# Three-stage kernel (attention, ELU block, gated block): order of products in the ELU block's Strassen pairs, weight-stream steps, token sums and gate differences

## The chip, the cores and the metric

One Trainium2 chip, one core of it. The metric is device time in microseconds (us), the median of several executions. The time of the kernel before is 675.72 us (median of 3 runs, 674.67 to 677.73).

## The reference

Three stages, all in float32:

- Attention with pooled queries: q, k, v are (2, 8, 1152, 64). Pairs of query rows are averaged, scores are scaled by 1/8, softmax, times v. The result, reshaped, is x with 1152 tokens of 512 features.
- First block ("MoE 1" in the kernel's names): h = x @ w_in (512 to 2048), g = h where h > 0, else exp(h) - 1, x2 = g @ w_out (2048 to 512).
- Second block ("MoE 2"): xn = x2 / rms(x2) * rms_g, out = (silu(xn @ w_gate) * (xn @ w_val)) @ w_out, with 1536 inner features.

## The kernel before, in words

**Split numbers.** TensorE multiplies numbers of reduced precision, so each operand is kept as a high part and a lower part (the number minus its high part), and each product is three matmuls: high by high, low by high, high by low (`product`, lines 216 to 218, and `Branch.group`, line 746). A high part is made by a cast, mostly on ACT; a lower part by a subtraction, on POOL (`lo_pool`, line 64) or DVE (`lo_dve`, line 70).

**Chunks and Strassen pairs.** Tokens are taken in three chunks of 384 columns (c = 0, 1, 2). For a pair of 128-wide weight blocks, chunks 0 and 1 together are one 2 by 2 block product done with seven half-depth products (numbers 1 to 7 in `Branch.m`, six matmuls each, line 746), and chunk 2 is done plainly (numbers 8 and 9, one for each weight block, twelve matmuls each). Several products add up in one PSUM bank: 2 goes on top of 1 (bank `a`), 7 and 4 on top of 6 (bank `b`), 3 on top of 5 (bank `e`). Between them a reader must have taken the intermediate value: after 1, ACT copies `a` to m1 (line 758) before 2 may write; after 6, DVE makes u2 = b + m1 (line 781); after 7, DVE makes u3 = b + m1 (line 787) before 4 may write. Products 5, 6, 7, 3 use sums of the weight blocks (s(1) to s(4), from `get_sums`), products 5, 6, 7, 4 use sums of the token blocks (`ts[0]` to `ts[3]`, made from t1, t2, t3, t4).

**Banks.** `bank()` hands out seven PSUM banks in turn, so an allocation waits for the readers of the one seven before it.

**First block.** 16 blocks of w_in and 16 of w_out, in four quarters q. Quarter 0 makes its four w_in blocks with plain products; quarters 1 to 3 are two Strassen pairs each, `Elu(2q)` and `Elu(2q + 1)`, run in an order written out by hand (`run`). Each output goes through `elu`: on ACT a relu (line 246) and an exp (line 247), on DVE a combination (line 248), on ACT a cast (line 249), on POOL the lower part. The last ones are put off by two and three calls of `flush`. After each quarter come rows m = 0 to 3 of w_out (`out1`), each for three chunks, whose results DVE adds into x2 (lines 855, 859).

**Weight stream.** `Stream.work` is a generator, and every `ws.step(i, k)` issues its next k steps between other work, so its place in the engines' queues is set by these counts. For each weight block of 512 KB: ACT takes its two words (line 120, which needs the load; line 122), ACT casts the block before (line 183), POOL makes that one's lower part, DVE puts the words together (lines 131, 133, 136). Line 136 frees a load buffer, of which there are two; SP starts the next load there. After the second block of a pair, POOL makes four sums (lines 156 to 162), ACT casts them (line 170) and POOL makes their lower part. A block has nine steps, a pair of blocks some six more.

**Token sums.** During quarter 0 `sums_from_x` makes the four differences on DVE (line 661), the casts on ACT (line 664), and the lower parts: of t1 and t4 on DVE, of t3 and t2 on POOL.

**Second block.** `Norm.sums`, `spread` and `scale` normalise a chunk (line 717 is a square root on ACT, 718 a reciprocal on DVE, 724 a transpose on TensorE, 730 to 732 scale, cast and split). The first pair of gate and value blocks is done plainly, as `unit(i, c)`: TensorE runs unit(0, 0), unit(1, 0) with the sums of chunk 2, unit(0, 1), the spread of chunk 2, unit(1, 1), unit(0, 2), unit(1, 2). `swiglu` follows a unit with Silu on ACT (line 930) and a product on DVE (line 932). Before the first Silu, ACT loads the table (line 948). The four gate differences t1, t3, t2, t4 are all made on DVE at line 939, right after unit(0, 0) is issued, and three casts (line 941) right after them. Ten Strassen pairs `Gate(2)` to `Gate(11)` follow, then w_out.

The order around the changed place in the second block, before:

```python
    for o, a, b in ((t1, b12, b11), (t3, b22, b12), (t2, b22, t1), (t4, b21, t2)):
        V.tensor_tensor(out=o, in0=a, in1=b, op=ALU.subtract)
    for n, t in ((2, t3), (1, t2), (3, t4)):
        T.copy(ts[n][0], t)
    lo_pool(ts[2][1], t3, ts[2][0])
    ws.step(wi, 4)
    first.append(unit(1, 0, norms[2].sums))
```

Of the kernel before, what the change touches and what calls it, by code (L numbers as in the profile page):

```python
# [12 lines left out]
ALU = mybir.AluOpType  # L13
# [26 lines left out]
def tile_kernel(ctx: ExitStack, tc: tile.TileContext, qd, kd, vd, w1d, w2d, wgd, wvd, wod, rgd, outd):  # L40
    nc = tc.nc
    V, G, T, PE, SP = nc.vector, nc.gpsimd, nc.scalar, nc.tensor, nc.sync
# [20 lines left out]
    def lo_pool(o, i, h):  # L63
        G.tensor_tensor(out=o, in0=i, in1=f(h), op=ALU.subtract)  # L64
# [4 lines left out]
    def lo_dve(o, i, h):  # L69
        V.tensor_tensor(out=o, in0=i, in1=f(h), op=ALU.subtract)  # L70
# [372 lines left out]
    def emit_x(p, xs, a=0, b=QS):  # L443
# [7 lines left out]
        else:  # L451
# [5 lines left out]
    wi = 0  # L457
    ge = tuple(gep.tile([128, NE, CH], F32R, name=f"ge{n}", tag=f"ge{n}") for n in "hl")
    ws = Stream([w for q in range(4) for w in w_in[4 * q:4 * q + 4] + w_out[4 * q:4 * q + 4]]
                + [w[2 * i + n] for i in range(6) for w in (wgd, wvd) for n in range(2)] + [wod[i] for i in range(12)])  # L460
# [31 lines left out]
    for n in range(ns):  # L492
        p, k = n // NPT, n % NPT
# [8 lines left out]
    t = ap.tile([128, 3, 384], F32, tag="p", name="rawq0", bufs=3).rearrange("p a b -> p (a b)")  # L502
    t = t.rearrange("p (u c) -> p u c", u=2)
# [75 lines left out]
    for step in range(ns):  # L579
# [25 lines left out]
        for u in jobs.get(step, []):  # L605
# [4 lines left out]
            n = order.index(u)  # L610
# [40 lines left out]
    def sums_from_x():  # L651

        r = x2.rearrange("p m c -> p (m c)")[:, NT:NT + 3072].rearrange("p (n k c) -> p n k c", n=4, k=2)
        b11, b12, b21, b22 = (r[:, n] for n in (0, 1, 3, 2))
        for b, j, l in ((b11, 0, 0), (b21, 1, 0), (b12, 0, 1), (b22, 1, 1)):
            h, x = (f(t[:, 2 * j:2 * j + 2, cs(l)]) for t in (xh, xl))
            V.tensor_tensor(out=b, in0=h, in1=x, op=ALU.add)
            yield
        t1, t2, t3, t4 = b11, b22, b12, b21
        for n, o, a, b in ((0, t1, b12, b11), (2, t3, b22, b12), (1, t2, b22, t1), (3, t4, b21, t2)):  # L660
            V.tensor_tensor(out=o, in0=a, in1=b, op=ALU.subtract)
            yield
        for n, t in ((0, t1), (2, t3), (1, t2), (3, t4)):
            T.copy(ts[n][0], t)
            yield
            (lo_dve if n in (0, 3) else lo_pool)(ts[n][1], t, ts[n][0])
            yield

    sums_of_x = sums_from_x()
# [143 lines left out]
    def run(order, limit, k=1):  # L813
        ws.limit = limit
        for br, m in order:
            br.m(m)
            ws.step(wi, 3 * k if m > 7 else k)
# [3 lines left out]
    wi = 0  # L821
    for i in range(4):
# [9 lines left out]
                next(sums_of_x)  # L832
        wi += 1

    for q in range(4):
        if q:
            old, b = None, Elu(2 * q)
            run([(b, k) for k in ((1, 8, 2, 9, 6, 5, 7) if q == 1 else (1, 6, 5, 8, 7, 2, 9))], 2 * q + 2)
            old, b = b, Elu(2 * q + 1)
            run([(b, 1), (old, 4), (b, 8), (old, 3)], 2 * q + 2)  # L840
            wi += 2
            run([(b, k) for k in ((9, 6, 5, 7, 2, 4, 3) if q == 1 else (6, 5, 2, 7, 9, 4, 3))], 2 * q + 3)
            ws.limit = 2 * q + 4
            wi += 2

        def out1(c, m, b, then=None, ks=range(4)):
            product(b, ws.get(8 * q + 4 + m), lambda k: g_block(c, k), True, True, ks)
            flush()
            if then:
                then()  # L850
            if ks[-1] < 3:
                return
            x = x2[:, m, cs(c)]
            if q:
                V.tensor_tensor(out=x, in0=b, in1=x, op=ALU.add)
                if q == 3:
                    norms[c].square(m)
            else:
                V.tensor_copy(x, b)

        if q < 3:
            banks = {}
            for m, ks in ((0, (0, 1)), (1, (0, 1)), (0, (2, 3)), (1, (2, 3)), (2, range(4)), (3, range(4))):
                for c in (2, 0, 1):
                    if (m, c) not in banks:
                        banks[m, c] = bank()
                    out1(c, m, banks[m, c], None, ks)
                    if q == 0 and (m, ks[0]) != (1, 2):
                        next(sums_of_x, None)
                        if (m, ks[0]) != (0, 0):  # L870
                            next(sums_of_x, None)
                    ws.step(wi, 6 if len(ks) > 2 else 4 if ks[0] else 3 * m)
                if ks[-1] == 3:
                    wi += 1
        else:
            banks = {}
            for n, (c, m) in enumerate([(0, 0), (0, 1), (0, 2), (0, 3), (1, 0), (1, 1)]):
                b = banks[c, m] = bank()
                out1(c, m, b, None, (0, 1))
                if n == 3:  # L880
                    T.activation(out=dummy, in_=eps, func=AF.Sqrt)
                ws.step(wi, 0 if n < 3 else 2)
            for c in range(3):
                for n in range(4):
                    b, ks = (banks[c, n], (2, 3)) if (c, n) in banks else (bank(), range(4))
                    out1(c, n, b, norms[c - 1].sums if c and n == 3 - c else None, ks)
                    if (c, n) in ((2, 0), (2, 3)):
                        norms[n > 0].spread()
                        norms[n > 0].scale()
                    ws.step(wi, ((2, 2, 2, 0), (1, 1, 3, 3), (3, 3, 3, 3))[c][n])  # L890
            wi += 4
# [28 lines left out]
    def unit(i, c, between=None):  # L920
        b = bank(), bank()
        for n in range(2):
            product(b[n], ws.get(2 * n + i + wi), xchunk(c), True, True)
            if between and n == 0:
                between()
        return i, c, *b

    def swiglu(i, c, pg, pv, k=4):
        s = u[c][:, i]
        T.activation(out=s, in_=pg, func=AF.Silu)  # L930
        ws.step(wi, k)
        V.tensor_tensor(out=s, in0=pv, in1=s, op=ALU.mult)
# [2 lines left out]
    first = [unit(0, 0)]  # L935
    b11, b12, b21, b22 = (x2[:, 2 * j:2 * j + 2, cs(l)] for j in range(2) for l in range(2))
    t1, t2, t3, t4 = b11, b22, b12, b21
    for o, a, b in ((t1, b12, b11), (t3, b22, b12), (t2, b22, t1), (t4, b21, t2)):
        V.tensor_tensor(out=o, in0=a, in1=b, op=ALU.subtract)  # L939
    for n, t in ((2, t3), (1, t2), (3, t4)):  # L940
        T.copy(ts[n][0], t)
    lo_pool(ts[2][1], t3, ts[2][0])
    ws.step(wi, 4)
    first.append(unit(1, 0, norms[2].sums))
# [2 lines left out]
    u = [up.tile([128, 12, CH], F32, name=f"u{c}", tag=f"u{c}") for c in range(2)]  # L947
    T.activation(out=dummy, in_=eps, func=AF.Silu)  # L948
    swiglu(*first[0], 2)
    lo_pool(ts[1][1], t2, ts[1][0])  # L950
    swiglu(*first[1], 3)
    units = [unit(0, 1)]
    norms[2].spread()
    norms[2].scale()
# [38 lines left out]
    b = Gate(2)  # L993
    run([(b, 1), (b, 8), (b, 9), (b, 2)], 2, 4, 2)
    run([(b, 6), (b, 5)], 2, 4)
    old, b = b, Gate(3)
    run([(b, 1), (old, 7)], 2, 4)
    for n in range(3, 11):
        if n > 3:
            old, b = b, Gate(n)  # L1000
            run([(b, 1), (old, 4), (b, 6), (old, 3)], n - 1, n + 2)
        else:
            run([(b, 6), (old, 4), (old, 3)], n - 1, n + 1)
        if n == 10:
            split_u(0, 0, 3)
        run([(b, k) for k in (5, 8, 7, 2, 9)], n, n + 3)
    old = b
    b = Gate(11)
    run([(b, 1), (old, 4), (b, 6), (old, 3)], 10, 12, 1)
# [86 lines left out]
```

## Time and profile before

| what | value |
|---|---|
| median of 3 runs | 675.72 us |
| the profiled execution, its time | 675.94 us |
| its span, first to last instruction | 674.2 us |
| TensorE (PE) busy | 661.6 us, 98% |
| VectorE (DVE) busy | 512.0 us, 76% |
| ScalarE (ACT) busy | 464.7 us, 69% |
| GpSimd (POOL) busy | 448.2 us, 66% |
| mean granted TensorE clock | 0.997 |

Times in the trace count from the span's start. Each line of a timeline has the start, the duration, the engine, the line of the kernel, the operation, output and inputs by the program's names, how many were merged, and in brackets how long the engine sat idle before it and what ended that. Matmul durations overlap, since matmuls are pipelined: the distance of two starts is what one costs. SP is the engine that starts the loads.

### The profile page before, as it was taken

Reading aid. Unit: us, or ns where it says so; the run is one execution under the profiler, and the core shown is the slowest. Engines: PE = TensorE matmul, PEld = TensorE weight load, DVE = VectorE, ACT = ScalarE, POOL = GpSimd, SP = SyncE. Lnnn points to the kernel's source line nnn. Section 1 sums busy time; section 2 is a strip of 40 time slices with the busy share of each in tenths; the row PEclk is TensorE's granted clock in tenths of the full one; section 3 lists DMA queues with packets and bytes.
Section 4 is the critical chain, followed back from the end, with each engine's and each line's share of the span. In section 5 each row is a group of like instructions: output and inputs, shape, how many; then the busy total and the mean of one; then the engine's idle time right before and its main releaser. Section 6 shows DMA issues by size and latency. Waiting matters only on the chain.

```text
span 674.2 us, 11387 instructions
## 1 busy us (share of the span) xinstructions
PE 661.6 (98%) x4149; PEld 652.9 (97%) x4149; DVE 512.0 (76%) x882; ACT 464.7 (69%) x910; POOL 448.2 (66%) x408
## 2 busy tenths in 40 slices
PE   8999999999999999989999999998999999999997
PEld 7999999999999999989999999998999999999997
DVE  7989989998999878886776877678687776776300
ACT  6888889898989868757758658755657654654300
POOL 5998898898988225876685785656979765413200
PEclk9999999999999999998999999999999999999999
DMA  5523333223233002142142241210323322204200
GB/s 175 181 94 96 138 126 112 90 89 120 89 123 103 1 1 95 38 150 90 66 134 87 73 147 62 68 59 32 124 95 126 126 72 84 94 1 142 85 36 35
DMA packets 21624, 61.75 MB, mean 92 GB/s; under 512 B 2752, under 2 KB 5056, under 8 KB 21568
## 3 DMA queue, kind: packets, MB, share of 16 engines
q1 hardware_dynamic: 21568, 61.03, 27.1%
q8 instruction: 32, 0.52, 0.3%
q14 instruction: 24, 0.20, 0.1%
HBM read 58.66 MB, written 2.36 MB: 91 GB/s over the span
## 4 chain that ended last, share of the span: by engine, by line
PE 50%; DVE 3%; ACT 2%; DMA 1%; issue 0%; DVEq 0%; ACTq 0%; SPq 0%
PE b L746 17%; PE b L216 11%; PE b L218 11%; PE b L217 11%; DMA wr<-in_w_dram 1%; DVE x L939 1%; DVE xl L70 1%; ACT xh L731 0%; DVE wt L136 0%; ACT we L120 0%; ACT wm L122 0%; DVE wm L133 0%; DVE wm L131 0%; ACT sqm L707 0%; ACT L948 0%
## 5 line engine op out<-in xcount | busy, mean ns | idle before, releaser
L64 POOL TENSOR_TENSOR wl<-wt,wh 128x512 fp32r<-128x512 f32 x68 | 91.5, 1347 | 75.0 <-ACT wh L183 73.9
L70 DVE TENSOR_TENSOR ptl<-t,pth 128x384 fp32r<-128x384 f32 x216 | 106.7, 548 | 5.0 <-ACT pth L375 4.4
L353 DVE TENSOR_SCALAR_CACHE_REDUCE p<-s 128x1152 f32<-128x1152 f32 x72 | 97.3, 1353 | 14.5 <-PE s L349 13.6
L375 ACT CAST pth<-t 128x384 fp32r<-128x384 f32 x216 | 89.1, 487 | 21.9 <-PE t L367 21.1
L349 PE MATMUL s<-kd,qt 128*128 128x384 f32 x480 | 98.6, 342 | 2.3 <-DVE p L353 1.8
L358 ACT ACTIVATE p<-p,st 128x1152 f32<-128x1152 f32 x72 | 91.4, 1270 | 0.5 <-DVE p L353 0.2
L216 PE MATMUL b<-xh,wh 128*128 128x384 f32 x260 | 88.4, 340 | 1.1 <-ACT u L930 1.1
L218 PE MATMUL b<-xh,wl 128*128 128x384 f32 x260 | 88.1, 339 | 0.0
L217 PE MATMUL b<-xl,wh 128*128 128x384 f32 x260 | 88.0, 339 | 0.0
L349 PEld LDWEIGHTS s<-kd,qt 128*128 128x128 f32 x480 | 81.0, 188 | 5.9 <-DVE p L353 2.5
L393 PE MATMUL o<-pth,vd 128*128 128x256 f32 (+1 forms) x288 | 84.4, 315 | 0.0
L367 PE MATMUL t<-ident,p 128*128 128x128 f32 x648 | 82.5, 273 | 0.0
L393 PE MATMUL o<-ptl,vd 128*128 128x256 f32 (+1 forms) x288 | 78.5, 295 | 0.0
L367 PEld LDWEIGHTS t<-ident,p 128*128 128x128 f32 x648 | 75.0, 141 | 2.0 <-ACT p L358 0.3
L120 ACT ACTIVATE we<-wr 128x512 uint32<-128x512 uint32 x68 | 45.4, 667 | 40.6 <-DMA wr<-in_w_dram 19.8
L131 DVE TENSOR_SCALAR wm<-wm 128x512 f32<-128x512 f32 x63 | 43.7, 694 | 20.3 <-ACT wm L122 20.3
L122 ACT ACTIVATE wm<-wr 128x512 f32<-128x512 f32 x63 | 39.4, 626 | 22.2 <-DVE wt L136 22.2
L393 PEld LDWEIGHTS o<-pth,vd 128*128 128x128 f32 x288 | 54.4, 189 | 0.3
L393 PEld LDWEIGHTS o<-ptl,vd 128*128 128x128 f32 x288 | 54.5, 189 | 0.0
L64 POOL TENSOR_TENSOR gl<-eg,gh 128x384 fp32r<-128x384 f32 x35 | 37.6, 1090 | 21.3 <-ACT gh L249 21.2
L216 PEld LDWEIGHTS b<-xh,wh 128*128 128x128 f32 x260 | 49.4, 190 | 1.4 <-ACT u L930 1.4
L217 PEld LDWEIGHTS b<-xl,wh 128*128 128x128 f32 x260 | 49.4, 190 | 0.0
(194 smaller groups left out, 1765.8 us busy)
## 6 DMA issues: line engine op xcount, KB each, us to landing
wr<-in_w_dram SPq DMA_DIRECT2D x32, 512.0 KB, 3.2
rawq<-in_q_dram SPq DMA_DIRECT2D x15, 576.0 KB, 4.1
rawk<-in_k_dram SPq DMA_DIRECT2D x28, 288.0 KB, 2.8
wr<-in_wg_dram SPq DMA_DIRECT2D x12, 512.0 KB, 3.2
wr<-in_wv_dram SPq DMA_DIRECT2D x12, 512.0 KB, 3.3
wr<-in_wo_dram SPq DMA_DIRECT2D x12, 512.0 KB, 3.2
rawv<-in_v_dram SPq DMA_DIRECT2D x16, 288.0 KB, 2.8
out_dram<-o SPq DMA_DIRECT2D x12, 192.0 KB, 1.8
```

What stands on the lines that cost most here:

```text
L64: G.tensor_tensor(out=o, in0=i, in1=f(h), op=ALU.subtract)
L70: V.tensor_tensor(out=o, in0=i, in1=f(h), op=ALU.subtract)
L216: PE.matmul(out, lhsT=wh[:, k, :], rhs=ah, start=first and k == 0, stop=False)
L217: PE.matmul(out, lhsT=wh[:, k, :], rhs=al, start=False, stop=False)
L218: PE.matmul(out, lhsT=wl[:, k, :], rhs=ah, start=False, stop=last and k == 3)
L349: PE.matmul(s[:, m, 0:384], lhsT=a, rhs=b[:, 384 * m:384 * m + 384], start=n == 0, stop=n == len(parts) - 1)
L353: V.tensor_scalar(out=pt, in0=s[:, :, 0:384], scalar1=-0.0625, scalar2=None, op0=ALU.mult, op1=ALU.min, accum_out=st[p][:, 0, TILES[i][4], :])
L358: T.activation(out=pt, in_=pt, func=AF.Exp, scale=-1.0, bias=st[p][:, 0, TILES[i][4], :], accum_out=st[p][:, 1, TILES[i][4], :])
L367: PE.transpose(ps[:, k, :], src[:, 128 * b:128 * b + 128], ident)
L375: T.copy(oh, re(ps))
L393: PE.matmul(self.o[:, 0:self.N], lhsT=v[:, b, :], rhs=(pth, ptl)[u][:, g["buf"], b, g["c0"]:320], start=self.n == 0, stop=self.n == 17)
L746: PE.matmul(out, lhsT=a[x][:, k, :], rhs=b[y][:, k, :], start=first and (k, x, y) == (0, 0, 0), stop=last and (k, x, y) == (1, 1, 0), skip ...
```

## The change

- Token sums of the first block: the lower parts of t3 and t2 are made on DVE as well, so all four are.
- First block, quarter 0: in w_out row m = 3 four stream steps follow each chunk, in place of six (twelve in all, before eighteen).
- First block, quarters 1 to 3: product 9 of the first pair of quarter 1 goes ahead of product 2; in its second pair 8 goes ahead of the old pair's 4, and 9 from the late part to between the old pair's 4 and 3. In quarters 2 and 3 the first pair runs 1, 8, 6, 5, 9, 7, 2 in place of 1, 6, 5, 8, 7, 2, 9; their second pairs are as before.
- Second block: only t1 and t3 are made where all four differences were; t2, with its cast, comes after the first `swiglu` and t4, with its cast, after the second. The lower part of t2 still comes ahead of the second `swiglu`, that of t4 still after the scaling of chunk 2.
- Second block, Gate(3): product 8 goes from the later run to between its 6 and the old pair's 4.

```diff
@@ -663,7 +663,7 @@
         for n, t in ((0, t1), (2, t3), (1, t2), (3, t4)):
             T.copy(ts[n][0], t)
             yield
-            (lo_dve if n in (0, 3) else lo_pool)(ts[n][1], t, ts[n][0])
+            lo_dve(ts[n][1], t, ts[n][0])
             yield
 
     sums_of_x = sums_from_x()
@@ -832,14 +832,17 @@
                 next(sums_of_x)
         wi += 1
 
+    orders = (((1, 8, 9, 2, 6, 5, 7), (1, 8, -4, 9, -3), (6, 5, 7, 2, 4, 3)),
+              ((1, 8, 6, 5, 9, 7, 2), (1, -4, 8, -3), (6, 5, 2, 7, 9, 4, 3)))
     for q in range(4):
         if q:
-            old, b = None, Elu(2 * q)
-            run([(b, k) for k in ((1, 8, 2, 9, 6, 5, 7) if q == 1 else (1, 6, 5, 8, 7, 2, 9))], 2 * q + 2)
+            early_part, middle, late_part = orders[q > 1]
+            b = Elu(2 * q)
+            run([(b, k) for k in early_part], 2 * q + 2)
             old, b = b, Elu(2 * q + 1)
-            run([(b, 1), (old, 4), (b, 8), (old, 3)], 2 * q + 2)
+            run([((b, old)[k < 0], abs(k)) for k in middle], 2 * q + 2)
             wi += 2
-            run([(b, k) for k in ((9, 6, 5, 7, 2, 4, 3) if q == 1 else (6, 5, 2, 7, 9, 4, 3))], 2 * q + 3)
+            run([(b, k) for k in late_part], 2 * q + 3)
             ws.limit = 2 * q + 4
             wi += 2
 
@@ -869,7 +872,7 @@
                         next(sums_of_x, None)
                         if (m, ks[0]) != (0, 0):
                             next(sums_of_x, None)
-                    ws.step(wi, 6 if len(ks) > 2 else 4 if ks[0] else 3 * m)
+                    ws.step(wi, (4 if q == 0 and m == 3 else 6) if len(ks) > 2 else 4 if ks[0] else 3 * m)
                 if ks[-1] == 3:
                     wi += 1
         else:
@@ -935,10 +938,9 @@
     first = [unit(0, 0)]
     b11, b12, b21, b22 = (x2[:, 2 * j:2 * j + 2, cs(l)] for j in range(2) for l in range(2))
     t1, t2, t3, t4 = b11, b22, b12, b21
-    for o, a, b in ((t1, b12, b11), (t3, b22, b12), (t2, b22, t1), (t4, b21, t2)):
+    for o, a, b in ((t1, b12, b11), (t3, b22, b12)):
         V.tensor_tensor(out=o, in0=a, in1=b, op=ALU.subtract)
-    for n, t in ((2, t3), (1, t2), (3, t4)):
-        T.copy(ts[n][0], t)
+    T.copy(ts[2][0], t3)
     lo_pool(ts[2][1], t3, ts[2][0])
     ws.step(wi, 4)
     first.append(unit(1, 0, norms[2].sums))
@@ -947,8 +949,12 @@
     u = [up.tile([128, 12, CH], F32, name=f"u{c}", tag=f"u{c}") for c in range(2)]
     T.activation(out=dummy, in_=eps, func=AF.Silu)
     swiglu(*first[0], 2)
+    V.tensor_tensor(out=t2, in0=b22, in1=t1, op=ALU.subtract)
+    T.copy(ts[1][0], t2)
     lo_pool(ts[1][1], t2, ts[1][0])
     swiglu(*first[1], 3)
+    V.tensor_tensor(out=t4, in0=b21, in1=t2, op=ALU.subtract)
+    T.copy(ts[3][0], t4)
     units = [unit(0, 1)]
     norms[2].spread()
     norms[2].scale()
@@ -1000,10 +1006,10 @@
             old, b = b, Gate(n)
             run([(b, 1), (old, 4), (b, 6), (old, 3)], n - 1, n + 2)
         else:
-            run([(b, 6), (old, 4), (old, 3)], n - 1, n + 1)
+            run([(b, 6), (b, 8), (old, 4), (old, 3)], n - 1, n + 1)
         if n == 10:
             split_u(0, 0, 3)
-        run([(b, k) for k in (5, 8, 7, 2, 9)], n, n + 3)
+        run([(b, k) for k in ((5, 7, 2, 9) if n == 3 else (5, 8, 7, 2, 9))], n, n + 3)
     old = b
     b = Gate(11)
     run([(b, 1), (old, 4), (b, 6), (old, 3)], 10, 12, 1)
```

## Rows read from the trace of the kernel before

**Rows 1.** The page's busy times: engine, us, share of the span, instructions.

```profile
PE 661.6 (98%) x4149; PEld 652.9 (97%) x4149; DVE 512.0 (76%) x882; ACT 464.7 (69%) x910; POOL 448.2 (66%) x408
```

**Rows 2.** Waits of PE over the span: us in total, times, longest.

```profile
PE b L746 <- ACT m L758: 3.0, 1, 3.0
...
PE b L216 <- ACT u L930: 1.1, 1, 1.1
PE b L724 <- DVE rr L718: 0.6, 1, 0.6
PE b L746 <- DVE u L787: 0.5, 1, 0.5
```

**Rows 3.** Timeline of PE, products 1, 8, 2, 9 of Elu(2), start of 6.

```profile
298.06 0.34 PE L746 MATMUL b<-xh,wh 128*128 128x384 f32 x1
...
301.01 0.34 PE L218 MATMUL b<-xh,wl 128*128 128x384 f32 x1
304.36 0.44 PE L746 MATMUL b<-xh,wh 128*128 128x384 f32 x1 [3.01 <-ACT m L758]
...
309.17 0.34 PE L746 MATMUL b<-tsh 128*128 128x384 f32 x1
```

**Rows 4.** Windows after that wait: busy us (count) by engine, then clock, DMA, GB/s.

```profile
305.40:308.75 3.35, 3.35 (x12) 3.35 (x11) 1.05 (x2) 1.96 (x3) 3.35 (x3) 0.50 0.34 103
```

**Rows 5.** Timeline of ACT in the same stretch.

```profile
302.22 0.66 ACT L120 ACTIVATE we<-wr 128x512 uint32<-128x512 uint32 x1 [1.76 <-DMA wr<-in_w_dram]
...
303.34 0.60 ACT L183 CAST wh<-wt 128x512 fp32r<-128x512 f32 x1
303.84 0.47 ACT L758 COPY m<-b 128x384 f32<-128x384 f32 x1
```

**Rows 6.** Timeline of POOL there, lower parts of the weight sums.

```profile
298.94 2.41 POOL L64 TENSOR_TENSOR tsl<-sf,tsh 128x1024 fp32r<-128x1024 f32 x1
...
306.64 2.37 POOL L64 TENSOR_TENSOR tsl<-sf,tsh 128x1024 fp32r<-128x1024 f32 x1
```

**Rows 7.** Timeline of DVE, lower parts of t1 and t4.

```profile
278.37 1.77 DVE L70 TENSOR_TENSOR xl<-x,xh 128x768 fp32r<-128x768 f32 x1
...
283.24 1.24 DVE L70 TENSOR_TENSOR tsl<-x,tsh 128x768 fp32r<-128x768 f32 x1
```

**Rows 8.** Timeline of POOL, lower parts of t3 and t2.

```profile
279.29 4.38 POOL L64 TENSOR_TENSOR tsl<-x,tsh 128x768 fp32r<-128x768 f32 x2
```

**Rows 9.** Timelines of PE and DVE, quarter 2, start of product 5 of Elu(5).

```profile
366.55 0.34 PE L746 MATMUL b<-tsh,tsl 128*128 128x384 f32 x1
366.96 0.44 PE L746 MATMUL b<-xh,tsh 128*128 128x384 f32 x1
...
366.35 0.55 DVE L248 SCALAR_TENSOR_TENSOR eg<-eg,b 128x384 f32<-128x384 f32 x1
```

**Rows 10.** The chain that ended last, gate differences: start, us, what.

```profile
457.73 0.97 DVE x L939
...
459.79 2.53 DVE x L939
```

**Rows 11.** Timeline of POOL beside the last difference.

```profile
459.64 1.85 POOL L64 TENSOR_TENSOR tsl<-x,tsh 128x768 fp32r<-128x768 f32 x1 [2.83 <-ACT tsh L941]
```

**Rows 12.** Timeline of ACT after the differences.

```profile
462.34 0.83 ACT L941 CAST tsh<-x 128x768 fp32r<-128x768 f32 x1 [1.71 <-DVE x L939]
...
463.60 0.26 ACT L717 ACTIVATE rr<-b,eps 128x3 f32<-128x3 f32 x1
463.87 1.28 ACT L948 ACT_TABLE_LOAD   x1
```

**Rows 13.** Timelines of DVE, POOL, PE: scaling of chunk 2, start of unit(0, 2).

```profile
466.72 2.18 DVE L730 SCALAR_TENSOR_TENSOR x<-x,rg,b 128x384 f32<-128x384 f32 x4
...
467.95 2.31 POOL L64 TENSOR_TENSOR xl<-x,xh 128x384 fp32r<-128x384 f32 x2 [1.12 <-ACT xh L731]
...
470.08 0.35 PE L216 MATMUL b<-xh,wh 128*128 128x384 f32 x1
```

## The prediction

> **What bounds the kernel now.** I read the busy times of the page first: TensorE (PE) is busy 661.6 of 674.2 us, 98% [rows 1], so the kernel can only gain where PE stands still or runs slowly. All PE idle time is 12.6 us. The second view was the list of PE's waits: behind the attention stage (whose waits the change doesn't touch) four stand out, 3.0 us on line 758, 1.1 and 0.6 us around the first units of the second block, 0.5 us on line 787 [rows 2]. Third came the timelines around each of them.
>
> The 3.0 us wait is in Elu(2). Product 1 starts at 298.06, product 8 ends its starts at 301.01 and product 2, which writes on top of 1, starts only at 304.36 [rows 3]. It waits for ACT's copy of the bank to m1. That copy takes 0.47 us and its data was there at 299.4 (six matmuls behind 298.06), but ACT runs in order, and ahead of it stood the first step of a weight block, which waited 1.76 us for its load and began at 302.22 [rows 5]. After the wait PE goes on at a granted clock of 0.50, the lower of its two levels (1.2 GHz), for the 3.35 us shown [rows 4], with nothing but the pause before it. So the price is more than 3.0 us: from 298.06 to the start of product 6 at 309.17 [rows 3] it takes 11.11 us for 36 matmuls, whose pitch at full clock is (301.01 - 298.06) / 17 = 0.174 us, 6.26 us in all. **4.85 us** are lost there.
>
> A measurement of this kernel can tell about 0.5%, 3.4 us, from no change.
>
> **The change, part by part.**
>
> *Product 9 ahead of 2, and fewer steps in row 3 (term A).* Now products 1, 8, 9, 2 follow each other: 2 is wanted at 298.06 + 30 x 0.174 = 303.3, where before it was wanted at 301.2. The steps matter as much: the row before Elu(2) issues six steps fewer, and counted back from the cast of line 183 at 303.34 these six are that cast, an empty step, lines 122 and 120 of the block that had to wait, and two more. So the copy to m1 now stands ahead of the waiting step, behind the cast of the block before it. Against that works a third edit: two lower parts of 1.24 us each (1.77 beside POOL) [rows 7] are added on DVE and leave POOL, where two took 4.38 [rows 8]. DVE is the engine that frees load buffers (line 136), of which there are two, so the loads behind come later by 2.5 us less what DVE idles there; I estimate 1.5 to 2.5 us. POOL's 4.38 us are no bottleneck there and are worth nothing by themselves. Working the chain through with that delay, the last cast ahead of the copy ends at about 302 to 302.7, and the copy at 302.4 to 303.2, against 303.3 wanted. It just holds. Next in line is product 6, now wanted at 298.06 + 36 x 0.174 = 304.3: its weight sums were ready at 298.94 + 2.41 = 301.35 [rows 6], with the delay 302.9 to 303.9, also just in time. Product 6 of Elu(3) is wanted at about 314.8; its sums were ready at 306.64 + 2.37 = 309.01 [rows 6] and now come six steps and four POOL operations of the outputs later, near 314.6. Three tight meetings, so I take off 0.35 us: **A = 4.5** (0 to 4.85).
>
> *Orders of quarters 2 and 3 (term B).* Product 5 of Elu(5) starts 366.96, where 366.55 + 0.174 would be 366.72, and the next after that at a slower first step: together 0.34 us. It takes the bank in which product 6 of Elu(4) was, whose last reader is line 248 at 366.35 to 366.90 [rows 9], queued on DVE behind work on the old pair's product 3. In the new order that seat in the rotation of seven belongs to product 8, read long before. The same happens once in quarter 3. What is late next: line 787 must be done before 4 writes, and between 7 and 4 there are now 12 matmuls (2.1 us) where there were 24; line 787 takes 0.55 us, so 1.5 us are left. **B = 0.7** (0 to 0.7). In quarter 1 the moved 8 and 9 lengthen the same distance and cost nothing: all products are the same, only their places change, and PE has no wait there now.
>
> *Gate differences (term C).* Four subtractions follow each other on DVE; alone one takes 0.97, the last took 2.53 [rows 10]. ACT's three casts (0.83) wait for them in order, and behind them stand the cast of a weight, the square root of chunk 2 at 463.60 and the table load of 1.28 us [rows 12], so both of PE's waits there (0.6 and 1.1, with the slow restart 1.85 us) come from the fourth difference. Now only t1 and t3 stand ahead. The subtraction of t3 ends at 457.73 + 0.97 = 458.7, its cast at 459.6, the weight's at 460.2, the square root at 460.5, the first Silu by 462.4, 3.2 us earlier: both waits go. But then DVE does: product of the first unit (to 462.9), t2 (463.9), then ACT's cast of t2 (464.7) and second Silu (465.2), DVE's product (465.7), t4. POOL takes the lower part of t2 from 464.7 to 466.6, beside t4. How a subtraction fares beside POOL is in the rows: the last one began at 459.79 and POOL's operation ran from 459.64 to 461.49 [rows 11]; it ended at 462.32, 0.83 us after POOL. So it stood almost still. t4 then ends at 467.5, or at 466.7 if it isn't held up, its cast 0.84 later, and ACT's casts of the scaled chunk 2 start 0.15 to 0.95 us later than before, where the scaling began at 466.72 [rows 13]. PE wants that chunk for unit(0, 2), 1.85 us earlier than the 470.08 of before. There was about 1 us of slack (POOL's two lower parts ended at 470.26, the later one wanted 1.2 us into the unit) [rows 13]. A new wait of 1.85 + 0.15 - 1.0 = 1.0 to 1.8 us stands there. **C = 0.3**, near the held-up end, since the one row of its kind shows it (0 to 1.85).
>
> The Trainium skill speaks here against the change: SBUF — State Buffer, section "SBUF: two separate sides", says that DVE and POOL share one pair of ports, that an operation of DVE with two SBUF inputs needs it against a POOL operation that reads SBUF, and that whoever starts first holds it for the whole instruction. By that rule t4 is held up fully and the sum below would be 6.1 us; without it 6.9. The trace agrees: 1.70 us of overlap, 1.56 us longer [rows 10, 11].
>
> *Gate(3) (term D).* Product 4 waits for line 787, 0.5 us [rows 2], with the slow restart 0.8. Twelve matmuls of product 8, 2.1 us, now stand between. Its bank was freed several products before. **D = 0.8** (0 to 0.8). Product 8 issues its six stream steps one group earlier; no engine is full there.
>
> **Sum.** 4.5 + 0.7 + 0.3 + 0.8 = 6.3 us. The profiled execution took 675.94 us (span 674.2 and 1.7 around it), 0.2 above the median, so I subtract from the median: 675.7 - 6.3 = **669.4 us**. All four terms at their upper ends give 8.2 us, 667.5.
>
> **The rivals.**
>
> *The wait shrinks and stays.* If the two lower parts on DVE cost the load chain the whole 2.5 us and more, the copy to m1 or one of the two weight sums is 1 to 2.5 us late. Half of A goes: 6.3 - 2.3 = 4.0, **671.7 us** (670.6 to 673). For it: all three meetings have under 1 us to spare. Against: ACT's copy no longer has a load ahead of it that isn't there yet.
>
> *The loads set the pace.* With each weight block taking its round through two buffers, PE would gain 5 us and wait for the next quarter's blocks. Only C and D stay: 675.7 - 1.1 = **674.6 us**. For it: ACT waits for a load in [rows 5]. Against: after 309 PE waits for no weight at all, and no weight wait stands in [rows 2].
>
> *Weight sums too late, slower.* The six steps held back put the sums of the second pair of quarter 1 behind the outputs of four products on ACT and POOL. Place: product 6 of Elu(3), wanted at 314.8. Each microsecond late is lost whole, and a pause of 3 us brings the half clock again (1.7 us). It decides from 4.6 us late, at 319.4, which with the 1.7 eats the 6.3. At 8 us, two more load rounds, the time is 675.7 - 6.3 + 9.7 = **679 us**. Against: I get 314.6 for them.
>
> **How the numbers follow.** Forecast 0.73 (its own range 667.5 to 670.8), shrunken wait 0.14, loads set the pace 0.08, slower 0.05. Faster by over 0.5% means under 672.3: the forecast and most of the second case, 0.73 + 0.11 = 0.84. Within 0.5%: 0.03 + 0.08 = 0.11. Slower 0.05. The range takes in the forecast's range and the shrunken wait up to 672.8; below, 667.3 stands for all terms full. About 0.17 is left out.
>
> **What would show it.** Right: no wait on line 758 in Elu(2), clock 1.00 through 300 to 312, products 1 to 6 in 6.3 us; no wait at product 5 of Elu(5) and Elu(7) or at 4 of Gate(2); no wait at line 724, but one of 1 to 2 us at the start of unit(0, 2). Wrong: a wait on line 758 or on the weight sums of over 1 us in quarter 1, a clock of 0.5 in any window after the start, or no new wait at unit(0, 2), which would put C near 1.85.

## The result, and the profile after

The changed kernel takes 670.64 us (median of 5 runs, 670.33 to 671.28); the kernel before took 677.18 in the runs beside it (5 runs, 674.67 to 678.0). The ratio is 0.9914, 95% interval 0.9891 to 0.9936: faster. The forecast was 669.4 us in a range of 667.3 to 672.8. The profiled execution of after took 670.6 us with a span of 668.8, 5.4 us less than the 674.2 of before.

The medians differ by 6.5 us, the two profiled executions by 5.4, because the kernel before varies, and its granted clock with it: of its 40 executions beside the experiments, 10 had a mean clock of 0.999 (674.39 to 675.39 us), 17 had 0.996 or 0.997 (676.03 to 677.11) and 13 had 0.992 to 0.995 (676.72 to 678.13). Its profiled execution had 0.997, with the one stretch of half clock of [rows 4]; after had 1.000 in all five.

First the page of after, its busy times, and the list of PE's waits (us in total, times, longest), which answer to [rows 1] and [rows 2].

```profile
PE 660.0 (99%) x4149; PEld 651.2 (97%) x4149; DVE 513.7 (77%) x884; ACT 465.0 (70%) x910; POOL 444.1 (66%) x406
```

```profile
PE b L746 <- ACT m L758: 0.8, 1, 0.8
...
PE b L746 <- DVE u L787: 0.3, 1, 0.3
```

Both waits are new ones at old lines: 0.8 us on line 758 is now in Gate(2), 0.3 us on line 787 in Elu(3). The waits for lines 930 and 718 are gone. (In after, the casts of line 941 are at 943, 953 and 957, the differences of line 939 at 942, 952 and 956, lines 930 and 932 at 933 and 935.)

Where the time went is best seen in the distances between PE's starts, stage by stage, worked out from the timeline of PE in each profiled execution (us). Attention before and the output product behind (62.93 us in both) hardly differ. The last stretch runs into w_out, up to its first product for chunk 2; "to w_out" means this place below too.

| stretch | before | after | e1 steps alone | e2 orders alone | e5 | e7 | e10 | e12 spread alone |
|---|---|---|---|---|---|---|---|---|
| Elu(2), Elu(3) | 27.88 | 23.95 | 24.08 | 24.26 | 24.04 | 23.09 | 23.09 | 29.21 |
| rows of quarter 1 | 25.08 | 25.09 | 25.08 | 25.44 | 25.09 | 25.08 | 25.09 | 25.09 |
| Elu(4), Elu(5) | 23.41 | 23.10 | 23.45 | 23.10 | 23.10 | 23.10 | 23.10 | 23.43 |
| rows of quarter 2 | 25.09 | 25.77 | 25.09 | 25.09 | 25.75 | 25.76 | 25.08 | 25.08 |
| Elu(6), Elu(7) | 23.40 | 23.10 | 23.44 | 23.10 | 23.10 | 23.10 | 23.10 | 23.44 |
| rows of quarter 3, first three units, to the spread | 41.20 | 40.33 | 40.33 | 41.18 | 40.32 | 40.32 | 40.33 | 40.43 |
| spread to unit(1, 1) | 1.68 | 0.24 | 1.18 | 1.68 | 1.18 | 0.25 | 1.19 | 0.24 |
| unit(1, 1) | 4.28 | 4.28 | 4.28 | 4.31 | 4.30 | 4.28 | 4.28 | 4.96 |
| unit(0, 2), unit(1, 2) | 8.35 | 8.99 | 8.35 | 8.35 | 8.35 | 9.04 | 8.35 | 9.60 |
| Gate(2) into w_out | 128.96 | 129.11 | 129.05 | 129.01 | 128.27 | 129.12 | 128.25 | 129.81 |

The column of after is 5.37 us shorter than that of before, which is the whole difference of the spans. Gained: 3.93, 0.31, 0.30, 0.87 and 1.44. Lost: 0.68 in the rows of quarter 2 and 0.64 at unit(0, 2). In the last stretch 0.80 is gained and 0.95 lost.

**Elu(2).** The timelines of PE and ACT in after, against [rows 3] and [rows 5], and the window that answers to [rows 4] (busy us with counts for PE, weight load, DVE, ACT and POOL, then clock, DMA share, GB/s):

```profile
298.08 0.34 PE L746 MATMUL b<-xh,wh 128*128 128x384 f32 x1
...
303.28 0.33 PE L746 MATMUL b<-xh,wh 128*128 128x384 f32 x1
...
299.26 0.67 ACT L120 ACTIVATE we<-wr 128x512 uint32<-128x512 uint32 x1
...
300.90 0.47 ACT L758 COPY m<-b 128x384 f32<-128x384 f32 x1
...
302.74 0.67 ACT L120 ACTIVATE we<-wr 128x512 uint32<-128x512 uint32 x1 [0.29 <-DMA wr<-in_w_dram]
```

```profile
303.35:306.70 3.35, 3.35 (x21) 3.35 (x20) 1.15 (x4) 3.29 (x9) 3.27 (x5) 1.00 0.41 157
```

Product 2 starts at 303.28, 5.20 us behind product 1, the 30 matmuls of 0.174 that were forecast. The copy to m1 is done at 301.37, and the step that waits for its load now stands behind it. The clock stays at 1.00.

**Elu(3), the give-back.** Products 7 and 4 now wait, 0.24 and 0.42 us beyond the pitch; the next start after each is 0.11 late too, 0.88 in all. PE and DVE of after:

```profile
317.17 0.44 PE L746 MATMUL b<-tsh 128*128 128x384 f32 x1
...
319.81 0.45 PE L746 MATMUL b<-tsh,wh 128*128 128x384 f32 x1 [0.26 <-DVE u L787]
...
315.97 0.69 DVE L131 TENSOR_SCALAR wm<-wm 128x512 f32<-128x512 f32 x1
316.57 0.55 DVE L781 TENSOR_TENSOR u<-b,m 128x384 f32<-128x384 f32 x1
...
318.61 0.68 DVE L136 SCALAR_TENSOR_TENSOR wt<-wr,wm 128x512 uint32<-128x512 uint32 x1
319.21 0.55 DVE L787 TENSOR_TENSOR u<-b,m 128x384 f32<-128x384 f32 x1
```

The readers of bank `b`, lines 781 and 787, each stand on DVE right behind an instruction of the weight stream (line 131, line 136). These are steps that the count in quarter 0 moved: e2, where the count is as before, has no wait at 7 or 4 here (e1, where it is changed alone, has both).

**Rows of quarter 2.** POOL and PE of after:

```profile
375.03 1.31 POOL L64 TENSOR_TENSOR wl<-wt,wh 128x512 fp32r<-128x512 f32 x1
376.27 2.99 POOL L64 TENSOR_TENSOR gl<-eg,gh 128x384 fp32r<-128x384 f32 x3
...
377.37 0.45 PE L217 MATMUL b<-gl,wh 128*128 128x384 f32 x1
```

A weight's lower part (1.31 us) stands on POOL ahead of three lower parts of the last outputs, and PE wants these in the rows: it waits at 377.37 and once more at 379.32, 0.68 us together with the restarts.

**First units.** DVE, POOL, PE and ACT of after:

```profile
460.15 1.83 DVE L956 TENSOR_TENSOR x<-x 128x768 f32<-128x768 f32 x1
...
459.33 1.84 POOL L64 TENSOR_TENSOR tsl<-x,tsh 128x768 fp32r<-128x768 f32 x1 [1.80 <-ACT tsh L953]
...
464.41 0.44 PE L217 MATMUL b<-xl,wh 128*128 128x384 f32 x1
...
479.05 0.44 PE L746 MATMUL b<-xh,wh 128*128 128x384 f32 x1 [0.76 <-ACT m L758]
...
478.53 0.47 ACT L758 COPY m<-b 128x384 f32<-128x384 f32 x1
```

t2 (line 952) takes 0.95 us alone; t4 (line 956) takes 1.83 beside POOL and ends at 461.98, 0.81 behind POOL's 461.17. The Trainium skill, SBUF — State Buffer, section "SBUF: two separate sides", says that between a DVE operation with two SBUF inputs and a POOL operation that reads SBUF, the one that came first holds the shared ports for its whole instruction; the trace agrees, since 0.81 of the 0.95 us was still to do. Two waits follow: the lower parts of chunk 2 at unit(0, 2) (464.41 and 465.70, 0.64 us together), and 0.93 us at product 2 of Gate(2), again on the copy to m1.

### The profile page after: what moved, and what is told of

Read it like the earlier page. It is cut to its first block, busy times and chain, and to the rows that moved or that the text cites. A ratio compares the mean times of both kernels' runs of the same rounds, so it can differ in the third digit from the quotient of the medians.

```text
span 668.8 us, 11390 instructions
## 1 busy us (share of the span) xinstructions
PE 660.0 (99%) x4149; PEld 651.2 (97%) x4149; DVE 513.7 (77%) x884; ACT 465.0 (70%) x910; POOL 444.1 (66%) x406
## 4 chain that ended last, share of the span: by engine, by line
PE 85%; POOL 6%; ACT 3%; DVE 3%; issue 1%; DMA 1%; SPq 0%; POOLq 0%; DVEq 0%; ACTq 0%
PE b L746 15%; PE b L217 12%; PE b L218 12%; PE b L216 12%; PE s L349 11%; PE o L393 10%; PE t L367 9%; POOL kd L64 1%; POOL qt L64 1%; POOL rawq L306 1%; DMA rawq<-in_q_dram 1%; PE t L432 1%; POOL gl L64 1%; POOL xl L64 0%; POOL qt L61 0%
## 5 line engine op out<-in xcount | busy, mean ns | idle before, releaser
L218 PEld LDWEIGHTS b<-xh,wl 128*128 128x128 f32 x260 | 48.8, 188 | 0.0
```

Source lines behind the costliest of these rows:

```text
L218: PE.matmul(out, lhsT=wl[:, k, :], rhs=ah, start=False, stop=last and k == 3)
```

## The experiments

Twelve kernels were run, each beside the kernel before on the same chip: its medians there were 676.1 us (e1 to e4), 676.43 (e5 to e8) and 676.58 (e9 to e12).

**e1: the steps alone**, on the kernel before.

```diff
-                    ws.step(wi, 6 if len(ks) > 2 else 4 if ks[0] else 3 * m)
+                    ws.step(wi, (4 if q == 0 and m == 3 else 6) if len(ks) > 2 else 4 if ks[0] else 3 * m)
```

> The kernel before with the step count alone changed (12 steps after the chunks of row 3 of quarter 0, not 18). Theory, place in ACT's queue: the copy to m1 of Elu(2) stands ahead of the step that waits for a load, ends near 300.9, product 2 is wanted at 301.2: no wait over 0.3 us there, clock 1.00, product 6 starts near 304.4; the time falls by 4 to 4.7 us. Rival, the order of products does it: without product 9 in between a wait of 2 us or more stays on line 758 and the time falls by under 2 us.

Measured: 671.19 us (670.9 to 671.64), ratio 0.9936 [0.9919, 0.9954]. In the trace this one number gives 5.0 of the 5.37 us (sum of its column, 304.33 against 309.33). The wait on line 758 is gone with product 2 still ahead of 9: the copy ends at 301.62. Products 7 and 4 of Elu(3) wait as in after (0.21 and 0.66, and the restarts). The surprise lies 150 us further on: the two waits ahead of unit(1, 1) shrink from 2.31 to 0.94 us, though no instruction there was edited. DVE of e1, and of the kernel before in the same place:

```profile
447.57 2.18 DVE L730 SCALAR_TENSOR_TENSOR x<-x,rg,b 128x384 f32<-128x384 f32 x4
449.67 1.85 DVE L70 TENSOR_TENSOR xl<-x,xh 128x384 fp32r<-128x384 f32 x2
451.44 6.45 DVE L939 TENSOR_TENSOR x<-x 128x768 f32<-128x768 f32 x4
```

```profile
450.67 2.18 DVE L730 SCALAR_TENSOR_TENSOR x<-x,rg,b 128x384 f32<-128x384 f32 x4
453.25 2.70 DVE L70 TENSOR_TENSOR xl<-x,xh 128x384 fp32r<-128x384 f32 x2 [0.39 <-ACT xh L731]
455.87 6.43 DVE L939 TENSOR_TENSOR x<-x 128x768 f32<-128x768 f32 x4
```

From the scaling of chunk 1 to the first difference it is 3.87 us in e1 and 5.20 before: the lower parts no longer wait 0.39 us for ACT's casts and take 1.85 in place of 2.70. ACT shows why. Before, two steps of the stream stood ahead of the casts, and the casts began 1.63 us behind the scaling; in e1 the steps stand behind the casts, and these begin after 0.64. Coming there earlier is not enough: e2 does so by 3.7 us, as e1 does by 3.9, and keeps both waits (41.18 and 1.68 us in the table). ACT of the kernel before, and of e1:

```profile
450.35 0.65 ACT L120 ACTIVATE we<-wr 128x512 uint32<-128x512 uint32 x1
450.91 0.62 ACT L122 ACTIVATE wm<-wr 128x512 f32<-128x512 f32 x1
...
452.30 1.74 ACT L731 CAST xh<-x 128x384 fp32r<-128x384 f32 x4
```

```profile
448.21 2.09 ACT L731 CAST xh<-x 128x384 fp32r<-128x384 f32 x4
450.20 0.67 ACT L120 ACTIVATE we<-wr 128x512 uint32<-128x512 uint32 x1
```

**e2: the orders alone** of Elu, on the kernel before.

```diff
+    orders = (((1, 8, 9, 2, 6, 5, 7), (1, 8, -4, 9, -3), (6, 5, 7, 2, 4, 3)),
+              ((1, 8, 6, 5, 9, 7, 2), (1, -4, 8, -3), (6, 5, 2, 7, 9, 4, 3)))
...
```

> The kernel before with the new orders of products in the Elu pairs alone. Theory, place in ACT's queue: the copy to m1 still stands behind the step that waits for its load and ends near 304.3, while product 2 is wanted at 303.3, so a wait of about 1 us stays on line 758; it is too short to bring the half clock; the waits at product 5 of Elu(5) and Elu(7) (0.34 us each) go; together 4 to 4.5 us less. Rival, the order alone covers the wait: none over 0.3 us on line 758 and 5 us or more less.

Measured: 672.51 us (672.3 to 672.99), ratio 0.9958 [0.9943, 0.9973]. PE of e2, and the window behind the wait:

```profile
304.48 0.44 PE L746 MATMUL b<-xh,wh 128*128 128x384 f32 x1 [0.89 <-ACT m L758]
```

```profile
304.40:307.70 3.30, 3.22 (x18) 3.22 (x19) 2.30 (x5) 2.96 (x7) 3.30 (x4) 1.00 0.53 170
```

The wait is still there, 0.89 us idle and 1.16 us beyond the pitch, but in the profiled execution the half clock isn't. So either edit alone takes most of the loss of Elu(2) and Elu(3): 3.80 us (e1), 3.62 (e2), both 3.93. The waits at product 5 of Elu(5) and Elu(7) go with the orders alone, and the rows of quarter 2 lose nothing, as they lose nothing in e1: it takes both edits for that. (The rows of quarter 1 lose 0.36 here.)

**e3: lower parts of t2 and t3 back on POOL**, from after.

```diff
-            lo_dve(ts[n][1], t, ts[n][0])
+            (lo_dve if n in (0, 3) else lo_pool)(ts[n][1], t, ts[n][0])
```

> The changed kernel with the lower parts of t3 and t2 back on POOL. Theory, this edit is worth nothing by itself: the loads come some 0.5 us earlier, no wait of PE appears in quarter 0, the time is that of the changed kernel within 0.7 us. Rival, the edit is needed: POOL's two lower parts delay the lower part of a weight block and PE waits for it in the rows of quarter 0, over 0.7 us more.

Measured: 670.9 us (670.47 to 671.3), ratio 0.9933 [0.9918, 0.9949], and no stretch differs from after by over 0.06 us. This edit is worth nothing, either way.

**e4: lower part of t2 behind the scaling**, from after.

```diff
-    lo_pool(ts[1][1], t2, ts[1][0])
...
     norms[2].scale()
+    lo_pool(ts[1][1], t2, ts[1][0])
```

> The changed kernel with the lower part of t2 moved on POOL behind the scaling of chunk 2, so that no POOL operation runs beside the subtraction that makes t4. Theory, the subtraction is held up by POOL: it takes 0.97 us, not 1.83, the scaling comes 0.86 us earlier, the 0.65 us wait at unit(0, 2) goes and the wait on line 758 in Gate(2), 1.04 us, shrinks to 0.2 to 0.4, since its load is started from the same chain on DVE; 1.2 to 1.5 us less than the changed kernel. Rival, the wait in Gate(2) is set by the load or by POOL's queue: it stays at 1 us or grows and at most 0.65 us is won.

Measured: 673.18 us (671.6 to 673.82), ratio 0.9956 [0.9939, 0.9973], so 2.5 us more than after by the medians where 1.2 to 1.5 less was expected. DVE, ACT and PE of e4, and the window from PE's restart:

```profile
461.01 0.95 DVE L955 TENSOR_TENSOR x<-x 128x768 f32<-128x768 f32 x1
...
474.47 1.05 ACT L170 CAST tsh<-sf 128x1024 fp32r<-128x1024 f32 x1 [4.02 <-POOL sf L162]
...
480.85 0.69 PE L746 MATMUL b<-xh,wh 128*128 128x384 f32 x1 [2.33 <-ACT m L758]
```

```profile
480.85:484.20 3.35, 3.35 (x11) 3.35 (x12) 1.66 (x3) 2.48 (x5) 3.35 (x4) 0.53 0.54 169
```

With nothing on POOL beside it t4 takes 0.95 us, and the wait at unit(0, 2) is gone (8.35): the hold-up is shown. But POOL now makes two lower parts in a row, the weight sums come later, ACT stands 4.02 us for them, and the copy to m1 in Gate(2) is behind: 2.33 us of wait, then half clock in the profiled execution, and Gate(2) to w_out takes 132.12. The rival of the expectation holds.

**e5: the four differences up front again**, from after (lines 939 and 941 as before, the rest as after).

```diff
-    for o, a, b in ((t1, b12, b11), (t3, b22, b12)):
+    for o, a, b in ((t1, b12, b11), (t3, b22, b12), (t2, b22, t1), (t4, b21, t2)):
         V.tensor_tensor(out=o, in0=a, in1=b, op=ALU.subtract)
-    T.copy(ts[2][0], t3)
+    for n, t in ((2, t3), (1, t2), (3, t4)):
+        T.copy(ts[n][0], t)
...
```

> The changed kernel with the four gate differences and their casts up front again, as before. Theory, the step count already took most of these waits: only about 0.9 us stays ahead of unit(1, 1), as with the step count alone, and the two waits that the spread brought (0.65 us at unit(0, 2), 0.9 us in Gate(2)) go, so the time is 0.4 to 0.8 us under the changed kernel's. Rival, the prediction's term C: the 2.2 us of waits at the spread of chunk 2 and at unit(1, 1) come back and the time is 0.5 us or more above the changed kernel's.

Measured: 670.4 us (669.81 to 670.9), ratio 0.9912 [0.9896, 0.9928]. Before unit(1, 1) there are 0.94 us of wait, at unit(0, 2) none, in Gate(2) the 0.93 is gone: 142.10 us from the spread to w_out against 142.62 in after. In after's own surroundings the spread loses 0.5 us; the medians can't tell the two apart. DVE of after, DVE and ACT of e5:

```profile
467.44 0.69 DVE L136 SCALAR_TENSOR_TENSOR wt<-wr,wm 128x512 uint32<-128x512 uint32 x1
```

```profile
467.18 0.69 DVE L136 SCALAR_TENSOR_TENSOR wt<-wr,wm 128x512 uint32<-128x512 uint32 x1
...
478.29 0.48 ACT L758 COPY m<-b 128x384 f32<-128x384 f32 x1
```

Counted from the start of quarter 3's rows (419.09 in after, 419.43 in e5), line 136 comes 0.60 us later in after and the copy to m1 0.58, while PE wants it 0.32 sooner: 0.90 of the 0.93 us of wait in Gate(2).

**e6 and e8: lower part of t4 on DVE**, from after; in e8 that of t2 also behind the scaling.

```diff
-    lo_pool(ts[3][1], t4, ts[3][0])
+    lo_dve(ts[3][1], t4, ts[3][0])
```

> The changed kernel with the lower part of t4, 2.15 us on POOL behind the scaled chunk 2, on DVE instead. Theory, POOL's queue sets the wait in Gate(2): the weight sums behind it come up to 2 us earlier, ACT's cast of them too, and the 0.93 us wait on line 758 falls under 0.3 us; the 0.65 us wait at unit(0, 2) stays; 0.6 to 0.9 us less than the changed kernel. Rival, DVE's chain to the next load sets it: DVE has 1.24 us more there, the wait stays or grows, the time is the same or up to 1.3 us more.

> The changed kernel with the lower part of t2 behind the scaling on POOL and that of t4 on DVE. Theory, both waits of the spread fall: t4's subtraction takes 0.97 us as nothing runs beside it, so no wait at unit(0, 2), and POOL has no more ahead of the weight sums than in the changed kernel, so the wait on line 758 in Gate(2) is at most the 0.93 us of the changed kernel and under 0.5 us if the earlier scaling helps it; 0.7 to 1.3 us less. Rival, DVE's 1.24 us delays the words of the next weight and the wait in Gate(2) grows past 1 us.

Measured: e6 674.09 us (672.51 to 674.45), 0.9963 [0.9948, 0.9978]; e8 674.41 (672.71 to 676.38), 0.9972 [0.9957, 0.9986]. Less than after was expected of both (by 0.6 to 0.9 and 0.7 to 1.3 us); both are slower by over 3 us by the medians. They lose at the copy in Gate(2), 2.63 and 3.18 us, and in half clock. DVE, ACT and PE of e6, and two windows after PE's restart:

```profile
466.03 2.04 DVE L70 TENSOR_TENSOR tsl<-x,tsh 128x768 fp32r<-128x768 f32 x1
...
469.45 0.69 DVE L136 SCALAR_TENSOR_TENSOR wt<-wr,wm 128x512 uint32<-128x512 uint32 x1
...
470.17 0.65 ACT L122 ACTIVATE wm<-wr 128x512 f32<-128x512 f32 x1 [4.02 <-DVE wt L136]
...
479.34 0.67 ACT L120 ACTIVATE we<-wr 128x512 uint32<-128x512 uint32 x1 [1.43 <-DMA wr<-in_wg_dram]
...
480.99 0.44 PE L746 MATMUL b<-xh,wh 128*128 128x384 f32 x1 [2.63 <-ACT m L758]
```

```profile
480.99:482.40 1.41, 1.41 (x7) 1.41 (x8) 1.28 (x3) 1.08 (x2) 1.41 (x3) 0.91 0.92 331
482.44:485.80 3.36, 3.36 (x13) 3.36 (x13) 1.75 (x4) 3.17 (x7) 3.00 (x3) 0.54 0.44 157
```

The 2.04 us on DVE push line 136 from 467.44 (after) to 469.45. Line 136 frees a load buffer: the next loads come later by as much, ACT waits for them in order, and the copy stands behind. So the stretch before Gate(2) has no room on DVE or on POOL.

**e7: second pair of quarter 1 in the order of the later ones**, from after.

```diff
-    orders = (((1, 8, 9, 2, 6, 5, 7), (1, 8, -4, 9, -3), (6, 5, 7, 2, 4, 3)),
+    orders = (((1, 8, 9, 2, 6, 5, 7), (1, 8, -4, -3), (6, 5, 2, 7, 9, 4, 3)),
```

> The changed kernel with quarter 1's second pair as 1, 8, old 4, old 3, then 6, 5, 2, 7, 9, 4, 3. Theory, the 0.9 us of waits in Elu(3) are distances: 6 to 7 and 7 to 4 have one product between and DVE stands behind a weight's step; with two and three products between, both waits go, 0.9 us less than the changed kernel. Rival, the sums of the second pair are the next bound: 6 is wanted 2.1 us earlier, at 312.7, where POOL ends their lower part at about 312.7, so a wait of 0.3 to 1 us appears there and under 0.5 us is won.

Measured: 669.45 us (669.43 to 670.04), ratio 0.99 [0.9884, 0.9916]. Elu(2) and Elu(3) take 23.09 us, without a wait: with 2 between 5 and 7, and 9 between 7 and 4, lines 781 and 787 have 12 matmuls of time, and 0.86 us come back.

**e9 and e10: both repairs, and then the steps moved.** e9 is e5 with e7; e10 is e9 with other step counts in the rows.

```diff
-                    ws.step(wi, (4 if q == 0 and m == 3 else 6) if len(ks) > 2 else 4 if ks[0] else 3 * m)
+                    ws.step(wi, (4 if q != 1 and m == 3 else 6) if len(ks) > 2 else 4 if ks[0] else 2 if q == 1 and m == 0 else 3 * m)
```

> The changed kernel with the four gate differences up front and with quarter 1's second pair as 1, 8, old 4, old 3, 6, 5, 2, 7, 9, 4, 3. Theory, the two repairs stand in different stages and add up: 0.9 and 0.6 us, 1.3 to 1.6 us less than the changed kernel, about 669.1. Rival, the earlier arrival at the second block brings the waits there back, as loads come no earlier: no better than the better of the two alone.

> The kernel with both repairs and the six held-back stream steps given back in quarter 1's first row and held back again in row 3 of quarter 2. Theory, the 0.68 us of waits on lower parts of the outputs in quarter 2's rows come from a weight's lower part that the six steps put among them on POOL: those waits go and the rest stays, 0.5 to 0.8 us less than with both repairs alone. Rival, the waits come from the new order of the pairs in quarter 2, whatever the steps: they stay, and the time is the same within 0.3 us or worse.

Measured: e9 669.27 us (669.2 to 669.35), 0.989 [0.9873, 0.9908]; e10 **669.07** (668.17 to 669.73), 0.9884 [0.9865, 0.9903], span 666.4. POOL of e10 in the rows of quarter 2:

```profile
374.27 2.97 POOL L64 TENSOR_TENSOR gl<-eg,gh 128x384 fp32r<-128x384 f32 x3 [0.90 <-ACT gh L249]
377.21 2.53 POOL L64 TENSOR_TENSOR wl<-wt,wh 128x512 fp32r<-128x512 f32 x2
```

The weights' lower parts now come behind the outputs', and the rows take 25.08 us again, where e9 has 25.72: the loss was the place of the steps. By its stretches e10 (301.86 us) is 2.10 better than after and 7.47 better than before. By the medians it is the fastest of all, but its interval touches that of after, and e9 and e10, 0.2 us apart where 0.5 to 0.8 was expected, can't be told apart by them.

**e11: Gate(3) in its old order**, from after.

```diff
-            run([(b, 6), (b, 8), (old, 4), (old, 3)], n - 1, n + 1)
+            run([(b, 6), (old, 4), (old, 3)], n - 1, n + 1)
...
-        run([(b, k) for k in ((5, 7, 2, 9) if n == 3 else (5, 8, 7, 2, 9))], n, n + 3)
+        run([(b, k) for k in (5, 8, 7, 2, 9)], n, n + 3)
```

> The changed kernel with product 8 of Gate(3) back in its later run. Theory, the distance between 7 and 4 of Gate(2) alone covers line 787: a wait of 0.8 us with its slow restart comes back there and nothing else, 0.6 to 0.9 us more than the changed kernel. Rival, the wait on line 758 that the changed kernel has just before gives line 787 its time: under 0.3 us more.

Measured: 672.02 us (671.57 to 672.22), ratio 0.9932 [0.9909, 0.9955]. The wait on line 787 is back, and Gate(2) to w_out takes 129.91 where after has 129.11: 0.80.

**e12: the spread of the differences alone**, on the kernel before (the second-block part of the change, without Gate(3)).

```diff
-    for o, a, b in ((t1, b12, b11), (t3, b22, b12), (t2, b22, t1), (t4, b21, t2)):
+    for o, a, b in ((t1, b12, b11), (t3, b22, b12)):
...
     swiglu(*first[0], 2)
+    V.tensor_tensor(out=t2, in0=b22, in1=t1, op=ALU.subtract)
+    T.copy(ts[1][0], t2)
...
```

> The kernel before with the gate differences spread and nothing else. Theory, where the six steps aren't held back, the spread takes the whole 2.3 us of waits at the spread of chunk 2 and at unit(1, 1) and gives back 0.6 to 0.7 us at unit(0, 2) and about 0.9 us in Gate(2): a net gain of 0.5 to 0.9 us. Rival, the prediction's price: 1.0 to 1.8 us given back at unit(0, 2) alone and nothing in Gate(2).

Measured: 676.84 us (675.37 to 677.73), ratio 1.0003 [0.9989, 1.0017]. PE of e12:

```profile
469.75 0.44 PE L216 MATMUL b<-xh,wh 128*128 128x384 f32 x1 [0.51 <-ACT xh L731]
470.83 0.44 PE L217 MATMUL b<-xl,wh 128*128 128x384 f32 x1 [0.64 <-POOL xl L64]
...
485.48 0.44 PE L746 MATMUL b<-xh,wh 128*128 128x384 f32 x1 [0.76 <-ACT m L758]
```

It takes away 2.21 us (0.77 and 1.44) and gives back 1.93 around unit(0, 2) and 0.85 behind it: from the rows of quarter 3 to w_out 185.04 us, where before has 184.47. The spread by itself wins nothing, where 0.5 to 0.9 us was expected. (Elu(2) and Elu(3), which e12 doesn't touch, took 29.21 in this execution: the wait on line 758 was 3.34 us, and the half clock behind it lasted 6.8 us.)

## Why the prediction was right, and where its steps were not

The sign, the main term and the range held. The terms forecast 6.3 us; the traces show 5.37: A and B came out 1.34 short together and C 0.42 long, and that these partly cancel is luck. That the medians differ by 6.54, close to 6.3, is luck too: executions of before lie up to 3.7 us apart with the clock, and the 4.85 us of term A is the loss of an execution with one stretch of half clock.

**A, forecast 4.5, measured 3.93.** The 4.85 us of Elu(2) went whole, by the mechanism named: fewer steps put the waiting load step behind the copy. Three things were off.
- The delay of the loads was put at 1.5 to 2.5 us. It was about 0.5 to 0.7: the step that waits for its load in [rows 5] began at 302.22 and begins at 302.74 in after, and DVE in after has

```profile
280.72 1.81 DVE L70 TENSOR_TENSOR tsl<-x,tsh 128x768 fp32r<-128x768 f32 x2
284.25 0.95 DVE L70 TENSOR_TENSOR tsl<-x,tsh 128x768 fp32r<-128x768 f32 x1
285.11 0.68 DVE L136 SCALAR_TENSOR_TENSOR wt<-wr,wm 128x512 uint32<-128x512 uint32 x1
```

  where line 136 was at 284.41 before. Three lower parts take 2.76 us, not 3.7, because POOL, relieved of its own, no longer stands beside them (1.24 in [rows 7] is a price beside POOL), and the rest fits into time in which DVE was idle. So the sentence that POOL's 4.38 us "are worth nothing by themselves" was wrong as a reason, and e3 shows that the whole edit is worth nothing either way.
- "Three tight meetings": none was missed. The copy had 1.9 us to spare, and the weight sums, ready at 301.89 and 312.72, were wanted at 304.32 and 314.84. The give-back of 0.88 came from a meeting that wasn't on the list: lines 781 and 787 on DVE. The held-back steps were followed on ACT and POOL only; three of a block's nine steps issue on DVE (lines 131, 133 and 136). The sentence that in quarter 1 the moved 8 and 9 "cost nothing" is right by e2: the steps cost it (e1), an order repairs it (e7).
- The two edits of A do the same work, 3.80 and 3.62 alone; the forecast added them to one term without saying what either gives alone.

**B, forecast 0.7, measured about -0.07.** The waits at product 5 went (0.31 and 0.30 by the stretches). The failing step is "what is late next": only line 787 was looked at. Late next were the last outputs' lower parts on POOL, in the rows behind the pair, 0.68 us. The prediction had counted the held-back steps only as far as Elu(3); they shift the stream in all the quarters behind, and it takes steps and orders together to lose this (e1, e2), and other steps to regain it (e10).

**C, forecast 0.3, measured 0.72.** Removed 2.31 us (forecast 1.85 with the restarts), given back 0.64 at unit(0, 2) (forecast 1.0 to 1.8) and 0.95 in Gate(2) (not forecast). The hold-up of t4 beside POOL is shown (1.83; 0.95 in e4). But the step that both of PE's waits come from the fourth difference failed: the step edit alone takes 1.37 of the 2.31 (e1), so these two gains were not C's. Taken alone the spread loses 0.57 (e12), put on top of the rest it loses 0.5 (e5 against after). The price of 1.0 to 1.8 at unit(0, 2) is near the 1.93 of e12, the case that it was worked out for. The other half of the price was missed because the prediction stopped at unit(0, 2): its steps end with the casts of chunk 2, and what these delay (the stream's steps, line 136 on DVE above all, and through its load the copy to m1) lies 15 us later.

**D, forecast 0.8, measured 0.80** (e11).

The rivals: the shrunken wait didn't come in after, though e2, where the steps stay ahead of the copy, is what it would have looked like; the loads didn't set the pace; the weight sums were in time.

## What to carry over

A count of steps that places a background stream is a phase: a change of six steps in one row moved waits in the next quarter's pairs, in rows 80 us later and in a stage 150 us later, in both directions, and was most of the gain. When such a count is changed, follow each of its instructions on every engine it uses (here ACT, POOL and DVE) up to the next place where PE waits for a reader in the same queue. With two edits for the same wait, run each alone before adding up; and a piece moved out of a full stretch must be followed past the first wait that it shortens, since the stretch behind pays.

## What the runs showed of the hardware

In the profiled executions the half clock, 1.2 in place of 2.4 GHz, followed pauses of PE of 2.33 (e4), 2.63 (e6), 3.01 [rows 3], 3.18 (e8) and 3.34 us (e12); behind pauses of 1.1 (in the kernel before, [rows 2]), 0.89 (e2) and less it didn't come. The wait of e2 cost 1.16 us and that of before 4.85. The half clock doesn't come in every execution: of the nine of e4 three had a mean clock of 1.000 and took 671.6 to 671.85 us, six had 0.997 and took 672.99 to 673.82. How long PE paused in the executions without a profile isn't known. The clock didn't fall at the same distance from the restart: in e4 it was at 0.53 from the restart on, in e6 PE ran 1.4 us at 0.91 first, and in the kernel before the half clock began about 1 us behind the restart [rows 3, 4].

A DVE operation with two SBUF operands beside POOL took as long as what was left of POOL's operation and nearly its own time: 0.95 became 1.83, and in Elu(3) line 248 became 2.35 us where the same operation takes 0.55 with POOL idle (at 359.39). DVE and POOL of after:

```profile
310.78 2.35 DVE L248 SCALAR_TENSOR_TENSOR eg<-eg,u 128x384 f32<-128x384 f32 x1
...
310.31 2.40 POOL L64 TENSOR_TENSOR tsl<-sf,tsh 128x1024 fp32r<-128x1024 f32 x1
```

DVE's operation ends at 313.13, 0.42 us after POOL's at 312.71. That hold-up is 1.8 us of DVE time in the middle of a pair. It is the rule in this trace: from 277 us on, 13 DVE operations with two SBUF operands start while POOL has over 0.1 us left of its own, and all end 0.41 to 0.43 us (384 columns) or 0.81 to 0.82 us (768 columns) behind POOL's. What the same work would cost with the lower parts of the sums elsewhere wasn't tried.
